# Attention and expert layer on one core: one clearing copy moved from ScalarE to VectorE, and the first 290 items in another order

## Chip, core and metric

The kernel runs on 1 core of one Trainium2 chip. The metric is device time in microseconds (us), the median of several runs, lower is better. Before the change it is 228.75 us (3 runs, 228.53 to 230.53). The engines are named as in the profile: PE (TensorE, matmuls; PEld its weight loads), DVE (VectorE), ACT (ScalarE), POOL (GpSimd) and SP, which only issues DMA transfers.

## What is computed

Causal attention over 4 batches and 8 heads (768 positions, head size 64). Three of the heads ("retrieval": 0, 2, 6) see all earlier positions, the other five only the first 4 positions and a window of 64. The result, 3072 tokens of 512, goes through a layer with a leaky rectifier with one slope per hidden column.

```python
scores = scale * np.matmul(q, k.transpose(0, 1, 3, 2))
...
scores = np.where(mask[None, :, :, :], scores, -1000000000.0)
scores = scores - np.max(scores, axis=-1, keepdims=True)
a = np.exp(scores)
a = a / (np.sum(a, axis=-1, keepdims=True) + 1e-09)
return np.matmul(a, v).astype(np.float32)
...
h = x @ w_in
g = np.maximum(h, 0.0) + alpha * np.minimum(h, 0.0)
return (g @ w_out).astype(np.float32)
```

## The kernel before

The work is cut into 16 attention segments (4 batches by 4 pairs of heads; segment n is pair n % 4 of batch n / 4) and 8 blocks of tokens for the expert layer (two per batch, 512 and 256 tokens). Each piece of work is an *item*: a name in a table with a function. One list, ORDER (line 14), names all 1076 items in the order in which they are emitted; nothing reorders them later. Each engine does its own instructions in that order and waits for the semaphores of what it reads; a bank of PSUM is taken and given back in that order as well. So a name's place in ORDER decides what stands ahead of it on its engine.

What the names mean (n a segment, t a block, i a number):

- `Lq`, `Lk`, `Lv` load q, k, v of a segment on SP's queue (functions load_q, load_k, load_rows, lines 203 to 250; the very first k load and the slopes' load `La` go on ScalarE's queue).
- `Cq`, `Ck`, `Cv` cast what was loaded to bf16. The letters in CQ, CK, CV (line 298) choose the engine: for segments 0 to 3 mostly P (GpSimd), later V (VectorE). `Cv` also copies the first four rows of a segment's values (`sinks`, line 306).
- `Tq`, `Tk` are transposes on TensorE (to_array, lines 354 to 363), `tq`, `tk` copy them out of PSUM into qT and kT (put_q, line 368; put_k, lines 386 to 394): with n of 1 to 3, `tq` on ScalarE and `tk` on VectorE; from 4, both on ScalarE; `tq0.0` on ScalarE, `tq0.1` on VectorE.
- `S` are score matmuls (lines 413 to 501), `s` their exponentials on ScalarE, `m` masks multiplied in on VectorE (from segment 4), `A` the matmuls with the values (line 552), `a` the division on VectorE (lines 562 and 563), `X`, `x` the transposition of the result into xT.
- `P` are the expert layer's first matmuls (line 597; a block's first units are cut in parts, as P0.1.0), `p` the relu on ScalarE (line 602), `g` the product with the slope on VectorE (line 609), `O`, `o` the second matmuls (line 617) and the output.
- `wi0` to `wi7` load w_in on GpSimd's queue (load_w_in, line 692; wi0 and wi1 hold the columns of units 0 to 3, wi6 and wi7 those of units 12 to 15), `wo0` to `wo3` load w_out (line 696).
- Clearing and constants: `zero`, `one`, `busy` and the fills `vz` (a column of values), `kz` (the transposed keys of segment slot i), `qz`, `sz`, `so`, `ro`, `vo`, `nz`, `kfz`, all memsets through line 288; `id` the identity; `idf` its copy in float32 (VectorE), read by `Al` (the transposition of the slopes on TensorE, line 651), whose result `al` turns into factors (line 655); `nms`, `nmr` the masks of segments 0 to 3 and `nr`, `ns` those of later ones (mr_near and ms_near, lines 659 to 677), all on GpSimd; `near0` to `near2` clear parts of the exponentials' buffers.
- `warm0` to `warm8` are matmuls of `busy` with itself whose result nobody reads (32, 3, 14 and six times 4 of them).

The keys' buffer kT_all is cleared by four items, because the streams' layout leaves gaps that the scores read: `kz0` and `kz1` by VectorE, `kz3` by GpSimd, and `kz2`, the slot of the third pair, by a copy on ScalarE from a broadcast zero.

Of the kernel before, what the change touches and what calls it, by code (L numbers as in the profile page):

```python
# [14 lines left out]
busy zero La id warm0 kz3 Lq0.0 sz1 vz2 nms nmr so1 vz0 Lq0.1 Lk1 warm8 warm5 warm3 kz1 qz0 one Lq1 Lk0 Ck0.0 kz2  # L15
Cq0.0 Tq0.0 tq0.0 Tk0.0 qz warm2 Lk2 kz0 tk0.0 Ck1.0 Ck1.1 Cq0.1 Tk1 S0.0.1 s0.0.1 Tq0.1 S0.0.0 Cq1 warm7 Lv0 tk1.0
sz2 vz1 vz3 Tq1 Lq2 Ck0.1 S0.0.2 s0.0.0 tk1.1 Tk0.1 Ck2.1 tq1 S1.1.0 s0.0.2 Ck2.0 warm4 tq0.1 nz0 s1.1.0 Cq2 tk0.1 Cv0
Lk3 S0.1.0 kfz0 Lv1 vo ro0 Ck3.1 s0.1.0 Lq3 Ck3.0 wi1 wi0 Cq3 sz0 idf S1.0.0 so2 Al s1.0.0 so0 al S0.1.1 s0.1.1 Lv2
Tq2 Tk2 tk2.1 tk2.0 S0.1.2 S1.0.1 A0.0 s0.1.2 a0.0 Cv1 A0.1 a0.1 Cv2 s1.0.1 tq2 S1.1.1 nz1 Tk3 S2.0.1 tk3.0 s1.1.1
S2.0.2 X0 s2.0.1 x0 wi6 s2.0.2 wi7 Lv3 Lq5 Tq3 tk3.1 S2.0.0 wi5 m4.0.2 warm6 S2.1.0 A1.0 a1.0 Lk4 s2.0.0 A2.0 S2.1.1  # L20
A1.1 a2.0 tq3 s2.1.0 a1.1 S3.0.0 s2.1.1 s3.0.0 A2.1 a2.1 S3.1.1 X1 S3.0.1 s3.0.1 Lk5 wi4 kfz2 Cv3.0 Cq5 Lk7 wi2 X2
Ck4.0 s3.1.1 S3.1.0 x1 P0.0.0 x2 P0.0.1 A3.0 P0.1.0 P0.1.1 Lk6 Lq4 Lq6 Ck4.1 kfz3 nr Cv3.1 s3.1.0 A3.1 Lv7 Lv5 Lq7
Ck5.0 wi3 a3.0 P0.2.0 Tq5 tq5 P0.3.0 P0.3.1 a3.1 X3 x3 ns kfz1 P0.2.1 Tk4 near2 P1.2 P0.1.2 P0.2.2 P0.0.2 p1.2 p0.1
g0.1 Ck5.1 P1.0 P0.3.2 g1.2 P0.15 tk4.0 p0.2 g0.2 p0.15 wo0 p1.0 Lk8 near0 g0.15 g1.0 ro1 P1.12 P1.14 m12.1.2 p0.0
g0.0 wo1 tk4.1 p1.12 P0.14 g1.12 p0.14 g0.14 P0.13 p0.13 g0.13 P0.11 p1.14 Tk5 Ck7.1 g1.14 P1.10 tk5.0 p0.11 p1.10
Ck6.0 Ck7.0 g0.11 m8.0.2 tk5.1 wo2 Lv6 Lv4 P0.10 P0.8 p0.8 Tk7 g1.10 wo3 Cq4 Lk9 P0.12 P1.8 p0.10 g0.8 p0.12 g0.10 Tq4
P0.6 P0.9 p0.3 Ck6.1 g0.3 tq4 P0.4.0 P0.5.0 Tk6 P0.4.1 p1.8 g1.8 tk7.0 p0.9 g0.9 Cq6 P0.5.1 P0.5.2 p0.5 g0.12 p0.6
tk6.1 P0.4.2 g0.6 g0.5 tk6.0 S4.0.5 P0.7 p0.7 P1.6 g0.7 P1.4 s4.0.5 p0.4 Tq6 m4.1.2 tk7.1 g0.4 Cv5 p1.6 g1.6 O0.1.0
tq6 S4.0.3 O0.2.0 O0.2.1 S5.1.1 S5.0.0 S4.0.1 S6.1.0 m14.0.2 p1.4 g1.4 s5.0.0 O0.1.1 s4.0.3 s4.0.1 O0.2.2 S5.0.2
S5.1.0 S4.0.2 S5.1.2 s6.1.0 m4.0.1 Cv7 O0.3.0 s5.0.2 s5.1.2 s5.1.1 s4.0.2 O0.1.2 s5.1.0 O0.1.3 o0.1 Cq7 Cv4 O0.3.1  # L30
m5.1.0 m8.1.2 m5.0.2 m4.0.3 m5.1.2 S4.0.0 S4.1.4 S5.0.1 S4.0.4 S4.1.0 s4.0.4 s5.0.1 Lk10 m5.0.1 O0.2.3 O0.3.2 Tq7
m5.0.0 o0.2 s4.1.0 m4.0.4 m5.1.1 A5.1 s4.0.0 m4.0.0 a5.1 O0.3.3 tq7 S7.0.0 S7.0.1 S4.1.3 S7.1.1 S6.0.5 S4.1.1 m4.0.5
s4.1.4 o0.3 Lq9 s4.1.3 Ck8 m4.1.3 A5.0 a5.0 X5 s4.1.1 A4.0 s7.0.0 s7.1.1 Lk11 Lq8 s7.0.1 a4.0 s6.0.5 near1 m7.0.0
m7.1.1 m4.1.0 O1.1.0 S7.1.0 S6.0.4 S7.0.2 S4.1.5 S6.0.1 S7.1.2 S6.1.1 O1.1.1 Cv6 s7.1.0 O1.0.0 s4.1.5 m7.0.1 s6.1.1
m4.1.5 m6.1.1 s7.1.2 m6.1.0 s7.0.2 m7.0.2 S6.0.2 S4.1.2 S6.1.2 S6.0.0 s6.0.4 s4.1.2 s6.0.1 s6.1.2 O1.0.1 m6.0.5 m7.1.0
m4.1.1 m4.1.4 m7.1.2 m6.1.2 S6.0.3 A4.1 s6.0.0 m6.0.0 m6.0.1 A7.1 O1.1.2 A6.1 s6.0.3 m6.0.4 m6.0.3 s6.0.2 a4.1 a6.1
A6.0 A7.0 a6.0 O1.1.3 O0.0.0 O0.0.1 O0.0.2 O1.0.2 m10.0.2 O1.0.3 O0.0.3 o0.0 X4 X6 a7.1 a7.0 X7 P2.9 P2.3 p2.9 P3.4
Ck9 Cq9 g2.9 P2.14 p2.14 g2.14 Cq8 p3.4 Lq10 Lq11 Dk8.0 P2.10 p2.10 Dk9.1 o1.0 p2.3 g2.3 g3.4 Dk8.1 P3.2 P3.14 P3.12
# [36 lines left out]
def kernel(  # L75
# [211 lines left out]
    def item(name, fn, *args):  # L287
        I[name] = lambda: fn(*args)  # L288
# [420 lines left out]
    for i in (0, 1):  # L709
        fill(f"kz{i}", kT_all[:, i].bitcast(fp32), 0.0)  # L710
# [137 lines left out]
```

## Time and profile before

| what | value |
| --- | --- |
| median of 3 runs | 228.75 us (228.53 to 230.53) |
| span of the profiled execution, first to last instruction | 227.4 us |
| granted TensorE clock | 1.000 |
| bytes moved by DMA | 37.39 MB |

The profile comes from one execution. Its span is 227.4 us; the time of a run has the launch around it as well, and no own time of the profiled execution is given. Busy time by engine in stretches of 10 us (length, PE, PEld, DVE, ACT, POOL with the number of instructions, clock, DMA share, GB/s):

```profile
0.00:10.00 10.00, 8.30 (x103) 7.54 (x104) 6.58 (x21) 5.34 (x6) 6.62 (x19) 1.00 0.86 243
10.00:20.00 10.00, 9.34 (x151) 8.13 (x149) 8.01 (x25) 8.97 (x13) 8.25 (x15) 1.00 1.11 247
20.00:30.00 10.00, 9.81 (x173) 8.50 (x172) 8.43 (x20) 5.99 (x10) 9.55 (x18) 1.00 1.18 245
30.00:40.00 10.00, 10.00 (x81) 6.92 (x79) 7.12 (x18) 7.88 (x14) 6.96 (x19) 1.00 1.18 248
40.00:50.00 10.00, 10.00 (x73) 6.01 (x72) 8.46 (x19) 9.54 (x23) 0.83 (x1) 1.00 1.21 203
50.00:60.00 10.00, 9.69 (x67) 4.75 (x65) 5.31 (x11) 9.01 (x24) 0.94 (x1) 1.00 1.11 219
```

A row says how much of a stretch each engine worked. Up to some 26 us the four segments of the first batch are loaded, cast, transposed and scored; from 26.8 on the expert layer's matmuls of the first blocks run beside the preparation of segments 4 to 7; the first scores of segment 4 come near 48 us. A line of the timelines gives start, busy time, engine, line, operation, output and input, and in brackets the idle time of the engine ahead of it and what ended it. A line of waits gives who waited for whom, with sum, number and longest.

### The profile page before, as it was taken

The page shows a single profiled execution, that of the slowest core. Times are in us where ns is not written, and L with a number is a line of the kernel's source. Part 1 is how long each engine was busy: PE and PEld are TensorE (multiplying, and loading weights), DVE is VectorE, ACT ScalarE, POOL GpSimd, SP SyncE. Part 2 cuts the span into 40 slices and gives each one's busy share as a digit, 9 for nine tenths or more (in the row PEclk, how much of TensorE's full clock was granted, in tenths as well). Part 3 has the DMA queues.
Part 4 walks back from the last instruction along what each step waited for, and adds up shares of the span by engine and source line. Part 5 has one row for each costly group of instructions (what it writes and reads, how often), then busy time and mean ns, then how long its engine had stood idle before and what let it go on. Part 6 is the DMA issues. An engine that isn't in the chain of part 4 may idle for free.

```text
span 227.4 us, 5240 instructions
## 1 busy us (share of the span) xinstructions
PE 221.6 (97%) x2005; PEld 135.3 (60%) x2005; DVE 150.0 (66%) x394; ACT 140.8 (62%) x285; POOL 46.0 (20%) x91
## 2 busy tenths in 40 slices
PE   8899999999999999999999999999999999999994
PEld 7789876664465657555556455556556555664454
DVE  5779849966379817899799119987586535866000
ACT  3889549999799028477994137787594236563311
POOL 6779995101130001000400001000110110000000
DMA  6999999999999598999969899995821420000213
GB/s 191 314 247 202 281 221 263 210 197 222 216 276 208 94 232 212 164 189 179 255 166 179 209 261 144 211 168 113 127 94 38 116 95 0 0 4 0 89 67 122
DMA packets 95417, 37.39 MB, mean 164 GB/s; under 512 B 82440, under 2 KB 93600, under 8 KB 95392
## 3 DMA queue, kind: packets, MB, share of 16 engines
q1 hardware_dynamic: 89136, 27.73, 61.8%
q0 software_dynamic: 5792, 8.93, 17.7%
q10 hardware_dynamic: 464, 0.40, 0.5%
q8 instruction: 15, 0.25, 0.4%
q14 instruction: 10, 0.08, 0.1%
HBM read 27.71 MB, written 6.29 MB: 150 GB/s over the span
## 4 chain that ended last, share of the span: by engine, by line
PE 90%; ACT 4%; DMA 2%; DVE 2%; issue 1%; ACTq 0%; DVEq 0%
PE P L597 35%; PE P L617 34%; PE P L552 7%; PE P L430 4%; PE P L413 2%; PE P L363 2%; DMA kf<-in_k_dram 2%; PE P L636 2%; ACT neg L602 1%; PE P L501 1%; ACT kT L288 1%; PE P L423 1%; PE P L577 1%; ACT kT L392 1%; DVE qT L368 0%
## 5 line engine op out<-in xcount | busy, mean ns | idle before, releaser
L609 DVE SCALAR_TENSOR_TENSOR g<-neg,oma,P 128x256 bf16<-128x256 f32 (+1 forms) x128 | 71.1, 608 | 36.0 <-ACT neg L602 35.5
L597 PE MATMUL P<-xT,w_in_b 128*128 128x512 bf16 (+1 forms) x512 | 86.5, 326 | 0.0
L617 PE MATMUL P<-w_out_b,g 128*128 128x512 bf16 x368 | 85.4, 379 | 0.0
L602 ACT ACTIVATE neg<-P 128x512 f32<-128x512 f32 x96 | 54.1, 600 | 27.1 <-PE P L597 22.6
L597 PEld LDWEIGHTS <-w_in_b 128*128 128x128 bf16 x512 | 49.5, 98 | 31.7 <-DVE g L609 0.2
L617 PEld LDWEIGHTS <-g 128*128 128x128 bf16 x368 | 33.7, 98 | 37.3 <-issue 1.2
L469 ACT ACTIVATE eR<-P 128x448 bf16<-128x448 f32 (+4 forms) x63 | 37.1, 636 | 5.3 <-PE P L430 2.5
L623 ACT COPY ot<-P 128x512 f32<-128x512 f32 x23 | 13.9, 603 | 37.3 <-PE P L617 32.4
L627 POOL DMA_DIRECT2D out_dram<-ot x18 | 10.3, 573 | 112.5 <-ACT ot L623 112.3
L517 ACT ACTIVATE eS<-P 128x352 bf16<-128x352 f32 x45 | 20.9, 494 | 3.7 <-PE P L430 3.7
L563 DVE TENSOR_TENSOR xn<-P,rcp 128x448 bf16<-128x448 f32 (+1 forms) x32 | 19.4, 608 | 1.1
L528 DVE TENSOR_TENSOR eS<-eS,ms_near 128x352 bf16<-128x352 bf16 x45 | 14.3, 335 | 4.6 <-ACT eS L517 4.5
L479 DVE TENSOR_TENSOR eR<-eR,mr_near 128x128 bf16<-128x128 bf16 (+5 forms) x54 | 11.2, 235 | 4.4 <-ACT eR L469 4.3
L413 PE MATMUL P<-qT,kT 128*128 128x192 bf16 (+14 forms) x68 | 11.3, 250 | 1.2 <-ACT qT L368 0.8
L430 PE MATMUL P<-qT,kT 64*128 64x176 bf16 (+13 forms) x181 | 11.8, 251 | 0.3 <-DVE g L609 0.3
L430 PEld LDWEIGHTS <-kT 64*128 64x128 bf16 x181 | 7.2, 94 | 7.6 <-issue 6.4
L552 PEld LDWEIGHTS <-eS 128*128 128x128 bf16 x260 | 9.6, 97 | 2.3 <-issue 0.6
L552 PE MATMUL P<-vb,eS 128*128 128x65 bf16 x260 | 10.8, 193 | 0.0
L562 DVE RECIPROCAL rcp<-P 128x7 f32<-128x7 f32 (+1 forms) x32 | 6.3, 198 | 6.8 <-PE P L552 6.6
L552 PE MATMUL P<-vb,eR 128*128 128x65 bf16 x276 | 10.1, 192 | 0.0
L552 PEld LDWEIGHTS <-eR 128*128 128x128 bf16 x276 | 9.4, 97 | 1.2
L645 DVE COPY ot<-P 128x128 f32<-128x128 f32 x1 | 0.3, 291 | 14.3 <-PE P L636 14.3
(96 smaller groups left out, 175.2 us busy)
## 6 DMA issues: line engine op xcount, KB each, us to landing
out_dram<-ot POOLq DMA_DIRECT2D x18, 256.0 KB, 3.5
kf<-in_k_dram SPq DMA_DIRECT2D x21, 192.0 KB
qf<-in_q_dram SPq DMA_DIRECT2D x18, 192.0 KB
vf<-in_v_dram SPq DMA_DIRECT2D x14, 196.0 KB
qf<-in_q_dram SPq DMA_DIRECT2D x7, 384.0 KB
vf<-in_v_dram SPq DMA_DIRECT2D x12, 192.0 KB
w_in_b<-in_moe_w_in_dram POOLq DMA_DIRECT2D x8, 256.0 KB, 9.7
w_out_b<-in_moe_w_out_dram POOLq DMA_DIRECT2D x4, 512.0 KB, 14.1
```

Source lines behind the costliest of these rows:

```text
L413: nc.tensor.matmul(to, keys, queries, start=True, stop=stop)
L430: nc.tensor.matmul(to, keys[own], queries[own], start=True, stop=True)
L469: nc.scalar.activation(ebuf[n, hh][:, lo:hi].rearrange("p (x c) -> p x c", x=len(parts)), P[:, got[0]:got[0] + len(parts), 0:(hi - lo) // ...
L517: nc.scalar.activation(slots, sc[:, 0:352].rearrange("p (s c) -> p s c", c=176), AF.Exp, scale=scale)
L528: nc.vector.tensor_tensor(slots, slots, ms_near[:, 0:2, :] if m == 0 else ms_near[:, 1:3, :], op=ALU.mult)
L552: nc.tensor.matmul(pav[:, i, :], e[:, o:o + 128], vv[:, j, hh, 0:D + 1], start=(m == 0), stop=(m == len(terms) - 1))
L563: nc.vector.tensor_tensor(xn[n][:, 0:nt, D * hh:D * hh + D], pav[:, :, 0:D], rcp.to_broadcast([128, nt, D]), op=ALU.mult)
L597: nc.tensor.matmul(psg[:, w * i:w * (i + 1)], w_in_b[:, c, 128 * fb:128 * (fb + 1)], xT[:, c, o:o + w], start=(x == 0), stop=(x == 3))
L602: nc.scalar.activation(neg[t, f], bank(held["P", t, f][0]), AF.Relu, scale=-1.0)
L609: nc.vector.scalar_tensor_tensor(g_buf[t % 2][:, fb, 0:w], neg[t, f][:, c], oma[:, fb:fb + 1], bank(got[0])[:, c], op0=ALU.mult, op1=ALU.add)
L617: nc.tensor.matmul(bank(held["O", t, s][0]), g_buf[t % 2][:, f, 128 * s:128 * (s + 1)], w_out_b[:, f, :], start=(f == 0), stop=(f == 15))
L623: nc.scalar.copy(ot, bank(got[0]))
```

## The change

`kz2` becomes a memset on VectorE like `kz0` and `kz1`. The part of ORDER ahead of `S4.0.5` (the first scores of segment 4), 290 items, is in another order; from `S4.0.5` on the order is the same. The same items are named. The loads on SP's queue keep their order among themselves, and so do the loads on GpSimd's queue. Places that differ, among others: `id` is behind `nz0`; `Cv1` is ahead of `wi1` and `wi0`, and `Cq3` between these; `vz1` is behind `tq0.1` on VectorE and `vz2` behind `al`; `idf` has `vo` ahead of it and no `so`; `Tk2` is ahead of `Al`; the first expert units are P0.1 and P0.3 instead of P0.0; `one`, `nr` and `ns` are last of the 290.

```diff
 ORDER = """
-busy zero La id warm0 kz3 Lq0.0 sz1 vz2 nms nmr so1 vz0 Lq0.1 Lk1 warm8 warm5 warm3 kz1 qz0 one Lq1 Lk0 Ck0.0 kz2
-Cq0.0 Tq0.0 tq0.0 Tk0.0 qz warm2 Lk2 kz0 tk0.0 Ck1.0 Ck1.1 Cq0.1 Tk1 S0.0.1 s0.0.1 Tq0.1 S0.0.0 Cq1 warm7 Lv0 tk1.0
-sz2 vz1 vz3 Tq1 Lq2 Ck0.1 S0.0.2 s0.0.0 tk1.1 Tk0.1 Ck2.1 tq1 S1.1.0 s0.0.2 Ck2.0 warm4 tq0.1 nz0 s1.1.0 Cq2 tk0.1 Cv0
-Lk3 S0.1.0 kfz0 Lv1 vo ro0 Ck3.1 s0.1.0 Lq3 Ck3.0 wi1 wi0 Cq3 sz0 idf S1.0.0 so2 Al s1.0.0 so0 al S0.1.1 s0.1.1 Lv2
-Tq2 Tk2 tk2.1 tk2.0 S0.1.2 S1.0.1 A0.0 s0.1.2 a0.0 Cv1 A0.1 a0.1 Cv2 s1.0.1 tq2 S1.1.1 nz1 Tk3 S2.0.1 tk3.0 s1.1.1
-S2.0.2 X0 s2.0.1 x0 wi6 s2.0.2 wi7 Lv3 Lq5 Tq3 tk3.1 S2.0.0 wi5 m4.0.2 warm6 S2.1.0 A1.0 a1.0 Lk4 s2.0.0 A2.0 S2.1.1
-A1.1 a2.0 tq3 s2.1.0 a1.1 S3.0.0 s2.1.1 s3.0.0 A2.1 a2.1 S3.1.1 X1 S3.0.1 s3.0.1 Lk5 wi4 kfz2 Cv3.0 Cq5 Lk7 wi2 X2
-Ck4.0 s3.1.1 S3.1.0 x1 P0.0.0 x2 P0.0.1 A3.0 P0.1.0 P0.1.1 Lk6 Lq4 Lq6 Ck4.1 kfz3 nr Cv3.1 s3.1.0 A3.1 Lv7 Lv5 Lq7
-Ck5.0 wi3 a3.0 P0.2.0 Tq5 tq5 P0.3.0 P0.3.1 a3.1 X3 x3 ns kfz1 P0.2.1 Tk4 near2 P1.2 P0.1.2 P0.2.2 P0.0.2 p1.2 p0.1
-g0.1 Ck5.1 P1.0 P0.3.2 g1.2 P0.15 tk4.0 p0.2 g0.2 p0.15 wo0 p1.0 Lk8 near0 g0.15 g1.0 ro1 P1.12 P1.14 m12.1.2 p0.0
-g0.0 wo1 tk4.1 p1.12 P0.14 g1.12 p0.14 g0.14 P0.13 p0.13 g0.13 P0.11 p1.14 Tk5 Ck7.1 g1.14 P1.10 tk5.0 p0.11 p1.10
-Ck6.0 Ck7.0 g0.11 m8.0.2 tk5.1 wo2 Lv6 Lv4 P0.10 P0.8 p0.8 Tk7 g1.10 wo3 Cq4 Lk9 P0.12 P1.8 p0.10 g0.8 p0.12 g0.10 Tq4
-P0.6 P0.9 p0.3 Ck6.1 g0.3 tq4 P0.4.0 P0.5.0 Tk6 P0.4.1 p1.8 g1.8 tk7.0 p0.9 g0.9 Cq6 P0.5.1 P0.5.2 p0.5 g0.12 p0.6
-tk6.1 P0.4.2 g0.6 g0.5 tk6.0 S4.0.5 P0.7 p0.7 P1.6 g0.7 P1.4 s4.0.5 p0.4 Tq6 m4.1.2 tk7.1 g0.4 Cv5 p1.6 g1.6 O0.1.0
...
+zero vz3 busy warm5 warm0 nz0 warm8 qz0 nms id qz vz0 sz1 so1 Lq0.0 Lq0.1 nmr Cq0.1 kz1 Lk1 Cq0.0 Tq0.0 Ck1.0 Lq1 La
+Lk0 ro0 Ck0.0 Tk0.0 warm2 Ck1.1 Cq1 kz0 tq0.0 kz2 Lk2 Ck2.0 Tk1 Ck0.1 Ck2.1 tk0.0 S0.0.1 m4.0.2 Lv0 s0.0.1 Tq0.1 Lq2
+S0.0.0 Tq1 tk1.1 kz3 S0.0.2 tk1.0 s0.0.0 sz0 Cv0 ro1 Cq2 kfz0 Lk3 Ck3.1 tq1 warm3 Ck3.0 tq0.1 Tk0.1 s0.0.2 vz1 Lv1 Cv1
+Lq3 S1.1.0 tk0.1 wi1 sz2 warm7 s1.1.0 vo S0.1.0 S1.0.0 Cq3 s0.1.0 Tk2 wi0 warm4 idf Al s1.0.0 tk2.0 S0.1.1 s0.1.1
+S0.1.2 s0.1.2 al A0.0 Tq2 tq2 S1.0.1 vz2 Lv2 s1.0.1 Cv2 A0.1 S1.1.1 a0.0 wi6 Tk3 s1.1.1 wi7 S2.0.1 S2.0.2 tk2.1 s2.0.1
+s2.0.2 a0.1 X0 so0 A1.0 S2.0.0 Tq3 Lv3 tk3.1 Cv3.0 x0 a1.0 so2 S2.1.0 Lq5 tk3.0 wi5 Lk4 warm6 s2.0.0 A2.0 s2.1.0
+S2.1.1 Cq5 A1.1 a2.0 tq3 s2.1.1 S3.0.0 A2.1 s3.0.0 S3.1.1 a1.1 Lk5 X1 s3.1.1 wi4 a2.1 S3.0.1 Lk7 x1 wi2 X2 S3.1.0
+near2 Lk6 x2 Cv3.1 P0.1.0 P0.1.1 Lq4 s3.0.1 A3.0 kfz2 Lq6 Lv7 s3.1.0 P0.3.0 Ck4.1 A3.1 Ck4.0 Lv5 P0.0.0 Lq7 P0.2.0
+P0.2.1 Tq5 a3.0 wi3 a3.1 X3 kfz3 Tk4 P0.3.1 x3 P1.0 P0.0.1 Ck5.1 P0.0.2 tq5 P0.2.2 p0.2 g0.2 P0.1.2 P1.2 p1.0 P0.15
+g1.0 tk4.0 p0.1 g0.1 P0.14 p1.2 wo0 g1.2 Lk8 wo1 P1.14 P0.3.2 p0.15 p0.0 P1.12 g0.15 p1.14 g1.14 g0.0 Ck5.0 p1.12 Tk5
+p0.14 Ck6.0 g0.14 Ck7.1 P0.13 m8.0.2 g1.12 tk4.1 tk5.0 p0.13 g0.13 wo2 P1.10 kfz1 p1.10 P0.10 Ck6.1 Lv6 P0.11 p0.10
+g0.10 Ck7.0 g1.10 tk5.1 p0.11 nz1 P1.8 P0.12 P0.8 p0.3 g0.11 Lv4 P0.6 p0.12 p0.6 wo3 Lk9 g0.3 g0.12 p1.8 g1.8 p0.8 Tk7
+Tk6 Cq4 Tq4 tq4 P0.9 P0.5.0 tk6.1 m12.1.2 g0.6 P0.4.0 P0.4.1 P0.5.1 P0.5.2 p0.9 g0.9 p0.5 tk6.0 Cq6 g0.5 g0.8 tk7.0
+near0 P0.4.2 one nr ns S4.0.5 P0.7 p0.7 P1.6 g0.7 P1.4 s4.0.5 p0.4 Tq6 m4.1.2 tk7.1 g0.4 Cv5 p1.6 g1.6 O0.1.0 tq6
...
-    for i in (0, 1):
+    for i in (0, 1, 2):
         fill(f"kz{i}", kT_all[:, i].bitcast(fp32), 0.0)
-    item("kz2", nc.scalar.copy, kT_all[:, 2].rearrange("p h c -> p (h c)"), zero.to_broadcast([128, 2 * 7 * 128]))
     fill("kz3", kT_all[:, 3].bitcast(fp32), 0.0, nc.gpsimd)
```

## Prediction

> **What bounds the kernel now.** I read the page first, then TensorE's waits in the first 60 us, the chain of waits over the start, the timelines of VectorE, GpSimd and ScalarE up to 60 us, and busy time by stretches. Two lines of the page, busy time and the chain that ended last:
>
> ```profile
> PE 221.6 (97%) x2005; PEld 135.3 (60%) x2005; DVE 150.0 (66%) x394; ACT 140.8 (62%) x285; POOL 46.0 (20%) x91
> PE 90%; ACT 4%; DMA 2%; DVE 2%; issue 1%; ACTq 0%; DVEq 0%
> ```
>
> TensorE sets the time. A reordering that gives it the same 2005 matmuls can win only what TensorE waits. Its waits in the first 60 us, with sum, number and longest:
>
> ```profile
> PE P L687 <- DVE zero L288: 1.1, 1, 1.1
> PE P L413 <- ACT qT L368: 0.8, 2, 0.5
> PE P L413 <- ACT eS L523: 0.4, 2, 0.2
> PE P L430 <- DVE g L609: 0.3, 1, 0.3
> PE P L651 <- DVE eS L288: 0.2, 1, 0.2
> ```
>
> Beside the start itself that is 1.7 us, all there is to win. What sets the first 0.5 us wait is in the chain of waits (start, length, what):
>
> ```profile
> 5.25 0.51 ACT g L328
> 5.77 1.58 ACT kT L288
> 7.35 0.70 ACT qT L368
> 8.05 0.04 issue
> 8.10 0.54 PE P L413 x3
> ```
>
> `kT L288` on ACT is `kz2`: the first scores (8.10) wait for `tq0.0`, which stands behind it. What would be next is in VectorE's timeline (start, busy, instruction, idle before), and ScalarE's load in the middle is in the stretches (PE, PEld, DVE, ACT, POOL):
>
> ```profile
> 6.38 1.01 DVE L386 COPY kT<-P 64x258 bf16<-64x258 bf16 x2 [1.71 <-PE P L361]
> 35.00:55.00 20.00, 19.69 (x142) 11.89 (x141) 16.45 (x34) 19.37 (x42) 3.18 (x5) 1.00 1.16 216
> ```
>
> From 35 to 55 us ScalarE works 19.37 of 20 us: there TensorE's lead is worth only what ScalarE can follow. GpSimd's rows around the first weight loads:
>
> ```profile
> 14.87 0.96 POOL L328 CAST g<-kf 128x384 bf16<-128x384 f32 x2
> 15.77 1.42 POOL L692 DMA_DIRECT2D w_in_b<-in_moe_w_in_dram  x2
> 17.17 0.85 POOL L315 CAST g<-qf 128x768 bf16<-128x768 f32 x1
> 17.94 0.95 POOL L348 CAST vb<-vf 128x896 bf16<-128x896 f32 x1
> 18.96 0.63 POOL L306 COPY vb<-vb 4x192 f32<-4x192 f32 x2
> ```
>
> **The change, part by part.** *kz2 to VectorE.* ScalarE loses a 1.68 us copy; VectorE gains a memset that its twin `kz1` does in 0.81. With the copy gone `tq0.0` can start at 5.77 and end by 6.5; next late is `tk0.0` on VectorE, 6.38 to 7.39, held by the key transposes and not by VectorE, which stood idle 1.71 us before it. The first scores then start at 7.39 plus the 0.05 from 8.05 to 8.10, that is 7.44 instead of 8.10: **-0.66**. Cover: before `tk0.0` VectorE now has `zero`, `vz3`, `busy`, `qz0`, `qz`, `vz0`, `sz1`, `so1`, `kz1` (0.06+0.17+0.11+0.38+0.11+0.17+0.22+0.14+0.81 = 2.2 from 0.90), the query cast (3.30 to 3.66, when its load lands), then `ro0` and two memsets (0.20+1.62): done near 5.5, 0.9 before 6.38. Without cover it would cost up to 0.81.
>
> *idf.* Before, `vo`, `ro0`, `sz2`, `idf` and two `so` stand between the key copies (end 12.53) and the slope transpose (13.99): 1.46 us with 0.30 of issue. After, `sz2`, `vo` and `idf` are left (0.22+0.12+0.71), and TensorE has six transposes and four warm-up matmuls to do ahead of it (chain: 0.34 and 0.22). I take the wait of 0.2 as gone: **-0.2** (bounds 0 and -0.2).
>
> *The scores of segments 0 to 3.* The other 0.25 of qT and the 0.4 of eS depend on which item follows which; new orders make new waits. Bounds 0 and -0.65; I take **-0.2**, nearer to nothing, since ScalarE has the same exponentials to do. So TensorE comes to the first expert matmul, 26.8 before, about 1.1 earlier, at 25.7.
>
> *The stretch bound by ScalarE.* Before, ScalarE's items up to the relu at 50.96 (the one behind the first scores of segment 4) come as relus in runs of one to four with q/k copies between; after, seven relus and later six stand in a row, and five copy groups (`tq4`, `tk6.1`, `tk6.0`, the cast `Cq4`, `tk7.0`) stand behind the six with two relus between. Before, the 16th relu ends at 44.61 and the marked one starts 6.35 later. After, behind the 18th relu stand 0.70 (44.58 to 45.28), 0.80 (45.77 to 46.57), two relus 1.0, 0.70 (50.26 to 50.96), 0.83 and 0.80: 4.85; and the 18th ends at least two units of expert matmuls later than the 16th, each four matmuls of 0.216 (chain: 12 in 2.59), 1.7 in all, and up to one set of transposes, 0.34. 4.85 + 1.7 to 2.1 is 6.6 to 6.9, against 6.35: +0.2 to +0.55. The run of seven can idle more: 7 times (0.86 - 0.55) is 2.2 if nothing is queued ahead. Bounds 0 and +2.2; I take **+0.6**, by the two rows that I could add up.
>
> *Masks late.* `one`, `nr` and `ns` move from near 28 us to just before the scores of segment 4. GpSimd does them in 1.25 (28.06) and 3.47 (30.33 to 33.80); behind `one`, near 51.5 by the row of the product that follows it, they end near 52.8 and 56.3. The first readers are at 56.49 (mr_near) and 59.8 (ms_near). Behind them on GpSimd waits `Cv5`, which starts at 56.11 on a load: nothing, up to 4.7 if the cover failed.
>
> *vz1 and vz2 late.* The value load of segment 1, issued at 9.68, waits for `vz1`, now behind `tq0.1` on VectorE: 10.61 - 0.66 + 0.96 + 0.17 = 11.1, so this load and every load behind it on SP's queue goes out 1.4 later. What hides it is the backlog: a query load issued at 6.26 was cast as it landed, at 13.08, 6.8 us, where the first took 2.5 (0.82 to 3.30): 4.3 queued ahead. Nothing; 1.4 without it.
>
> *GpSimd's queue.* `ident` is made behind `nz0` and `nms`, near 4.0, before its first use at 5.2. The w_out loads go out a few us earlier or as before: nothing, either way. `kz3`, `kfz1`, `nz1` and the warm-up groups only trade places beside other work: nothing. `wi1` and `wi0` are behind `Cv1` now: nothing in my sum, and the first rival.
>
> Sum: -0.66 - 0.2 - 0.2 + 0.6 = -0.46. The span of 227.4 becomes 226.9; the median of 228.75 has 1.35 around that span, so **228.3**. Of the shown runs (228.53, 228.75, 230.53) two lie within 0.2 of each other and one 1.8 above.
>
> **Rivals.** *First expert weights late (slower).* `wi1` and `wi0` were issued at 15.77 and 16.55 and landed 5.8 and 7.3 later. Now `Cv1` with its two small copies (0.95+0.63) stands ahead, and the query cast (0.85) between them. `Cv1` can't start before its load lands, between 13.1 (the query load ahead of it) and 17.2 (the one behind it was cast then), nor before GpSimd is free, 15.8. So `wi0` goes out at 15.8+0.95+0.63+0.65+0.85 = 18.9, or 1.2 later; with 7.3 it lands at 26.2 to 27.4, with the 8.7 of the quickest later one at 27.6 to 28.8. TensorE needs it at 25.7. The price is 0.5 to 3.1, total 228.8 to 231.4, in the middle 230.2. Against: with 5.8 it lands at 24.7 and costs nothing, and the transfers run in a saturated queue (DMA share over 1 from 5 us on), where what starts later needs not end as much later. It decides from a landing at 25.7 on.
>
> *ScalarE follows.* If the run of relus finds its banks full, nothing of the 1.06 is given back: 227.7. For: VectorE, which frees the banks, works only 16.45 of the 20 us. Against: ScalarE's 19.37 of 20.
>
> *The clock rises one period later.* The first 44 warm-up matmuls took 4.20 us, the next 14 took 0.96: TensorE starts at half rate and, from 4.4, 3.3 us after its first matmul, runs at full rate. The first matmul now waits for `busy` as the third memset, 0.2 later, and 40 instead of 44 come before the first transposes. If full rate came only at 7.7, up to half of 3.3 less the 0.26 idle is lost at the first scores, 1.4: 229.7. For it speaks only that the start moves; that the rate rose 3.3 us after the start speaks against. The Trainium skill ("TensorE: Matmul & The Clock Gate", Part 1: The HAM clock gate) says that the window which releases the clock runs freely, about 3.4 us long, so that a later start can miss one; the 3.3 us here agree with its length, and one profile can't show its phase.
>
> *The edit is not what it says:* both programs hold the same items and the same loads, so only the order and one engine differ; no chance.
>
> **Chances.** Forecast 0.50 (its own range 227.6 to 229.2); weights late 0.27; ScalarE follows 0.12; clock 0.06; a wait that I don't see 0.05. 227.2 to 231.2 leaves out a tail of `ScalarE follows` and the upper end of the late weights and the unseen. 1% is 2.3 us, about what a measurement of this kernel can tell from no change. Faster by that needs more than all of TensorE's 1.7 us: 0.06. Slower by it needs the upper third of the late weights, 0.12, or an unseen wait or two together: 0.22. Within: 0.72.
>
> **What would show it.** After: no ScalarE `kT` row at 5.77, the first scores near 7.45, no wait at L651, the first expert matmul near 25.7 with no wait for `w_in_b` (otherwise the first rival), the relu ahead of segment 4's first exponential at 50.4 to 50.6, no VectorE wait on `mr_near` or `ms_near`, first full-rate matmuls near 4.5. A landing of `wi0` after 26, a VectorE stall on a key cast, or a mask that is read late would make the forecast wrong.

## The result, and the profile after

The changed kernel takes 231.45 us (median of 12 runs, 231.09 to 232.94), the kernel before on the same chip 229.72 us (12 runs, 228.53 to 230.64). The ratio is 1.0078, with a 95% interval of 1.0053 to 1.0103: slower by 0.8%, where 228.3 us and no measurable change were forecast. The profiled run took 231.09 us with a span of 229.2 us, against 227.4 before; the granted clock is 1.00 in both. Some single runs of the versions below had a granted clock of 0.991 to 0.993 and took longer, among them three of the splice with the changed start and two with the early masks; by the means without them these two ratios would be near 1.005 and 1.006, not 1.0067 and 1.0073.

Two lines of the page of the changed kernel, busy time and the chain that ended last:

```profile
PE 222.1 (97%) x2005; PEld 134.9 (59%) x2005; DVE 151.6 (66%) x395; ACT 139.3 (61%) x284; POOL 46.4 (20%) x91
...
PE 80%; DMA 8%; ACT 4%; DVE 3%; POOL 2%; issue 1%; ACTq 0%; SPq 0%; POOLq 0%; DVEq 0%
```

TensorE's share of the chain fell from 90 to 80%, and transfers went from 2 to 8%: the way to the end now runs through loads. TensorE's waits in the first 60 us (sum, number, longest):

```profile
PE P L687 <- DVE busy L288: 1.2, 1, 1.2
PE P L597 <- DMA w_in_b<-in_moe_w_in_dram: 0.9, 1, 0.9
PE P L413 <- DVE kT L386: 0.4, 1, 0.4
PE P L430 <- DVE g L609: 0.3, 1, 0.3
PE P L363 <- POOL natm L328: 0.3, 1, 0.3
```

The first expert matmul in TensorE's timelines, before and then after (start, busy, instruction, and in brackets the idle time ahead of it):

```profile
26.80 0.81 PE L597 MATMUL P<-xT,w_in_b 128*128 128x512 bf16 x3
27.02 0.81 PE L597 MATMUL P<-xT,w_in_b 128*128 128x512 bf16 x3 [0.93 <-DMA w_in_b<-in_moe_w_in_dram]
```

The waits on `qT` and on the slopes (L651) are gone, as forecast. New are the first expert matmul's wait for its weights (0.9) and a transposition's for a key cast (0.3). The chain of waits of the same kernel shows where they come from (start, length, what):

```profile
10.02 0.96 DVE qT L368
10.98 0.07 issue
11.05 0.18 DVE vf L288
11.23 0.02 issue
11.24 0.37 SPq L246
11.61 0.04 issue
11.66 4.43 DMA vf<-in_v_dram
16.09 0.03 POOLq L348
16.12 0.08 issue
16.20 0.95 POOL vb L348
17.14 0.05 issue
17.20 0.63 POOL vb L306 x2
17.83 0.73 POOL w_in_b L692
18.56 0.83 POOL g L315
19.39 0.57 POOL w_in_b L692
...
20.65 9.41 DMA kf<-in_k_dram
30.07 0.05 issue
30.12 0.97 POOL natm L328 x2
```

`tq0.1`, then `vz1`, then the value load of segment 1 on SP's queue, its cast `Cv1`, and behind that `wi1`, `Cq3` and `wi0`. `wi0` is issued at 19.32 instead of 16.55 and lands at 26.88 instead of 23.81 (both landings from the transfers' semaphores in the trace). TensorE had finished the scores ahead of the expert matmuls at 26.1.

ScalarE's load in the stretch from 35 to 55 us is still near full, 18.84 of 20 us (length, PE, PEld, DVE, ACT, POOL with instructions, clock, DMA share, GB/s):

```profile
35.00:55.00 20.00, 19.79 (x140) 11.97 (x139) 16.46 (x34) 18.84 (x42) 8.64 (x17) 1.00 1.19 221
```

One more loss was not foreseen. It is in VectorE's timelines, before and then after (start, busy, instruction):

```profile
62.85 0.59 DVE L528 TENSOR_TENSOR eS<-eS,ms_near 128x352 bf16<-128x352 bf16 x2 [1.81 <-ACT eS L517]
64.03 1.36 DVE L528 TENSOR_TENSOR eS<-eS,ms_near 128x352 bf16<-128x352 bf16 x2 [1.75 <-ACT eS L517]
```

Beside the second row, in GpSimd's timeline of the changed kernel:

```profile
64.00 0.94 POOL L348 CAST vb<-vf 128x896 bf16<-128x896 f32 x1 [0.95 <-DMA vf<-in_v_dram]
```

The pair of mask products takes 1.36 us, where before it took 0.59. `Cv4` on GpSimd had started 0.03 earlier. The same steps in both profiles give the account (us from the start of the span):

| step | before | after | difference |
| --- | --- | --- | --- |
| first exponential (L469) | 8.73 | 7.80 | -0.93 |
| last retrieval exponential of segments 0 to 3 | 20.51 | 19.86 | -0.65 |
| first expert matmul (L597) | 26.80 | 27.02 | +0.22 |
| first retrieval exponential of segment 4 | 51.45 | 52.61 | +1.16 |
| a later retrieval exponential, behind these mask products | 65.82 | 67.65 | +1.83 |
| end of the span | 227.4 | 229.2 | +1.8 |

The lead at the start is there. Of it 0.3 is lost by 20 us; 0.9 is lost from there to the first expert matmul, 0.9 up to segment 4 and 0.7 at 64 us; from then on the two profiles run in parallel.

### The profile page after: what moved, and what is told of

Read it like the earlier page. It is cut to its first block, busy times and chain, and to the rows that moved or that the text cites. A ratio compares the mean times of both kernels' runs of the same rounds, so it can differ in the third digit from the quotient of the medians.

```text
span 229.2 us, 5247 instructions
## 1 busy us (share of the span) xinstructions
PE 222.1 (97%) x2005; PEld 134.9 (59%) x2005; DVE 151.6 (66%) x395; ACT 139.3 (61%) x284; POOL 46.4 (20%) x91
## 4 chain that ended last, share of the span: by engine, by line
PE 80%; DMA 8%; ACT 4%; DVE 3%; POOL 2%; issue 1%; ACTq 0%; SPq 0%; POOLq 0%; DVEq 0%
PE P L617 33%; PE P L597 33%; DMA kf<-in_k_dram 6%; PE P L552 6%; PE P L430 4%; DMA vf<-in_v_dram 2%; ACT neg L602 2%; PE P L636 2%; DVE kT L392 1%; DVE eS L528 1%; PE P L423 1%; POOL vb L348 1%; ACT kT L392 1%; POOL w_in_b L692 1%; PE P L363 1%
## 5 line engine op out<-in xcount | busy, mean ns | idle before, releaser
L597 PE MATMUL P<-xT,w_in_b 128*128 128x512 bf16 (+1 forms) x512 | 86.1, 326 | 1.0 <-DMA w_in_b<-in_moe_w_in_dram 0.9
L597 PEld LDWEIGHTS <-w_in_b 128*128 128x128 bf16 x512 | 49.4, 98 | 34.2 <-issue 1.5
L469 ACT ACTIVATE eR<-P 128x448 bf16<-128x448 f32 (+4 forms) x63 | 37.0, 634 | 6.5 <-PE P L462 2.7
L528 DVE TENSOR_TENSOR eS<-eS,ms_near 128x352 bf16<-128x352 bf16 x45 | 15.0, 350 | 4.7 <-ACT eS L517 2.3
```

Source lines behind the costliest of these rows:

```text
L469: nc.scalar.activation(ebuf[n, hh][:, lo:hi].rearrange("p (x c) -> p x c", x=len(parts)), P[:, got[0]:got[0] + len(parts), 0:(hi - lo) // ...
L528: nc.vector.tensor_tensor(slots, slots, ms_near[:, 0:2, :] if m == 0 else ms_near[:, 1:3, :], op=ALU.mult)
L597: nc.tensor.matmul(psg[:, w * i:w * (i + 1)], w_in_b[:, c, 128 * fb:128 * (fb + 1)], xT[:, c, o:o + w], start=(x == 0), stop=(x == 3))
```

## The experiments

Theory: `vz1` behind `tq0.1` and `Cv1` ahead of `wi1`, `wi0` make the first weights late. Rivals: the later order (ScalarE's stretch, the masks), the clock, and a start whose lead is worth nothing. Ratios are to the kernel before on the same chip, with 95% intervals.

**The memset alone.**

```diff
-    for i in (0, 1):
+    for i in (0, 1, 2):
         fill(f"kz{i}", kT_all[:, i].bitcast(fp32), 0.0)
-    item("kz2", nc.scalar.copy, kT_all[:, 2].rearrange("p h c -> p (h c)"), zero.to_broadcast([128, 2 * 7 * 128]))
```

> The kernel before with one edit: kz2 is a memset on VectorE instead of a copy on ScalarE; no item changes its place. Theory (the clearing copy did hold the first scores, and the loss of the changed kernel is all in the other order): the first scores start near 7.45 us instead of 8.10, as they do in the changed kernel (7.37 for the second key copy there against 7.60), and TensorE keeps most of the 0.66, so the span is 226.8 to 227.1 and the ratio to the kernel before 0.997 to 0.9985. Rival (a lead at the start is worth nothing, because loads and the first expert weights set when TensorE goes on): 227.4, ratio 1.000, with the 0.66 back as new waits before 27 us. Second rival (VectorE needs the time and the memset delays the key copies): ratio above 1.001.

Ratio 1.0003 (0.9973 to 1.0033). First scores at 7.61, but then this wait of TensorE:

```profile
PE P L363 <- DVE kT L394: 0.5, 1, 0.5
```

A transposition waits for VectorE's key copies. Of 0.49 at the first exponential 0.15 is left from 16 us on, and that is kept to 66 us. The time shows no gain, which neither excludes nor shows 0.15.

**Which half.** A splice: the first 161 items in the changed order and the rest of the items ahead of `S4.0.5` (they are 291, not 290) as before. And the opposite one.

> A splice: the first 161 items, up to the first expert matmul, in the changed order, and the other items up to the first scores of segment 4 in the order before. kz2 is the memset. It asks in which half the loss lies. Theory (both halves lose: late weights and keys by the first, ScalarE's order by the second): the wait for w_in_b of 0.9 stays, the stretch from 44 to 56 us gives its 0.4 to 0.6 back, and the collision of 0.8 us at 64 us may come or go with the phase: span 227.9 to 228.8, ratio 1.002 to 1.006. If the first half were all of it: 229.2, ratio 1.007 to 1.008. If the second half were all of it: below 227.4, ratio under 1.000.

> The opposite splice: the first 161 items in the order before, with kz2 as a memset on VectorE, then the other items up to the first scores of segment 4 in the changed order. Theory (both halves lose): no wait for w_in_b, the first expert matmul near 26.1 to 26.5 us; the stretch from 44 to 56 us costs 0.4 to 0.6, the masks made late cost nothing by themselves; span 227.0 to 228.0, ratio 0.999 to 1.003. If the second half held all of the loss: 229 or more, ratio above 1.006. If the first half held it all: that of the kernel before with the memset alone, below 227.1, ratio under 0.999.

Changed start: 1.0067 (1.0037 to 1.0096), with a wait of 1.1 for `w_in_b`. Start before: 1.0013 (0.9983 to 1.0042), no such wait. So most of the loss lies in the first half. The second half costs something in the profiles as well. From the first expert matmul to segment 4's first exponential, four profiles with the changed order there and no wait for a load on the way take 24.87 to 24.88 us, and four with the order before take 24.43 or 24.44 (all eight lack the record of that first matmul, so each is 0.2 longer in truth). A lead from the start is not kept by either order: the splice with the start before has 0.91 at the last exponential of segments 0 to 3 (19.60) and 0.13 at segment 4's first (51.32), and a version below with the order before loses 0.78 on the same way.

**Cv1 behind the weights.**

```diff
-vz1 Lv1 Cv1
+vz1 Lv1
...
-Tk2 wi0 warm4
+Tk2 wi0 Cv1 warm4
```

> The changed kernel with one item moved: Cv1, the cast of segment 1's values on GpSimd, stands behind wi0 and no longer ahead of wi1 and wi0. Theory (the first weights are late because their issue waits for this cast, as the chain of waits has it): wi1 goes out near 15.6 us instead of 17.79 and wi0 before 17.5 instead of 19.32, the wait of 0.9 us of the first expert matmul for w_in_b is gone, and about 0.5 to 0.9 us of span with it (228.3 to 228.7, ratio to the kernel before near 1.005). Rival (the key cast natm, which follows a load that landed at 30.07, is late in any case and takes back what is won): no wait for w_in_b, but the wait for natm grows from 0.3 to about 1.2 and the span stays within 0.2 of 229.2, ratio 1.007 to 1.008. Second rival (the transfers are saturated, and weights that start earlier land as late): the wait for w_in_b stays above 0.6.

1.0090 (1.0055 to 1.0125), a miss. The wait for `w_in_b` is gone, but the values' matmuls now wait for this cast:

```profile
PE P L552 <- POOL vb L348: 0.7, 1, 0.7
...
PE P L552 <- POOL vb L306: 0.2, 1, 0.2
```

GpSimd is not short of time there; its queue is held. `Cq3` still stands between `wi1` and `wi0`, and its load comes late, as GpSimd's timeline shows:

```profile
17.80 0.83 POOL L315 CAST g<-qf 128x768 bf16<-128x768 f32 x1 [1.49 <-DMA qf<-in_q_dram]
```

GpSimd stands idle for 1.49 us, `wi0` goes out at 18.57 (the forecast was before 17.5), and `Cv1` starts at 19.20, though its values landed at 16.16.

**vz1 early, and Cq3 behind wi0 as well** (the last pair of lines in the second kernel alone).

```diff
-m4.0.2 Lv0
+m4.0.2 vz1 Lv0
...
-s0.0.2 vz1 Lv1 Cv1
+s0.0.2 Lv1 Cv1
...
-S1.0.0 Cq3 s0.1.0 Tk2 wi0 warm4
+S1.0.0 s0.1.0 Tk2 wi0 Cq3 warm4
```

> The changed kernel with one item moved: vz1, the memset of segment 1's value buffer, stands ahead of Lv0 on VectorE (behind tk0.0) and no longer behind tq0.1. Theory (the 1.4 us for which SP's queue stands still pass through the value load, the cast Cv1 and the weight loads behind it to the first expert matmul): the value load of segment 1 goes out near 9.2 to 9.8 us instead of 11.24 and lands near 15.0; Cv1 starts when GpSimd is free, 15.6, instead of 16.20; wi0 goes out near 18.7 instead of 19.32 and lands near 26.2; the key load behind goes out 1 to 3 us earlier and natm is not waited for. The wait for w_in_b falls from 0.9 to 0.2 to 0.5 and the first relu from 33.41 to 32.6 to 33.0; span 228.2 to 228.9, ratio to the kernel before 1.003 to 1.006. Rival (the backlog of the queue hides the late issue, as the prediction had it): the loads land as in the changed kernel, within 0.3 us, and the span stays at 229.0 to 229.4, ratio 1.007 to 1.008.

> The changed kernel with vz1 ahead of Lv0 and also Cq3, the query cast between the two weight loads on GpSimd, behind wi0. Cv1 stays ahead of wi1. Theory (both the stalled queue and the work between the weight loads make wi0 late): wi1 goes out near 17.2, wi0 near 17.9, landing near 25; no wait for w_in_b at all, no wait for vb, and the first expert matmul starts at 25.3 to 26.2 by the phase of the clock; first relu 32.3 to 32.6; the rest of the way costs what it costs in the changed kernel: span 227.6 to 228.4, ratio 1.000 to 1.004. Rival (weights wait for the transfer queue and not for their issue): the wait for w_in_b stays above 0.6 and the ratio at 1.006 or more.

1.0056 (1.0030 to 1.0081) and 1.0050 (1.0030 to 1.0070). With `Cq3` behind, `wi0` goes out at 18.50 and lands at 27.05, against a forecast near 25 and no sooner than in the changed kernel. In the first of the two the weights land at 28.25 and TensorE waits longer than in the changed kernel, against the forecast: some of the first loads of that run landed up to 1 us later. Both ratios are lower than the changed kernel's 1.0078, but the intervals overlap, so a gain is likely and not shown.

**Both suspects undone, with the later order of either kernel.**

```diff
-m4.0.2 Lv0
+m4.0.2 vz1 Lv0
...
-s0.0.2 vz1 Lv1 Cv1
+s0.0.2 Lv1 wi1 wi0 Cv1
...
-tk0.1 wi1 sz2
+tk0.1 sz2
...
-Tk2 wi0 warm4
+Tk2 warm4
```

> The changed kernel with its two suspects undone: vz1 ahead of Lv0, and wi1, wi0 ahead of Cv1, with Cq3 behind all three on GpSimd. Theory (the start loses by late weight issues and a stalled load queue): wi1 goes out near 15.6, wi0 near 16.3, landing 23.5 to 25; Cv1 runs near 17 and ends in time for the values' matmuls; no wait for w_in_b and none for vb; the first expert matmul starts when TensorE gets there (25.3 to 27 us by the phase at which the clock rises). Mean span of the runs 228.1 to 228.6, against 228.8 with vz1 and Cq3 alone, 229.6 of the changed kernel and 227.9 of the kernel before: ratio 1.001 to 1.003. What is left would be the later order. Rival (what is left lies in the later order alone, the weights are done with at 17.9): 228.8, ratio 1.004 to 1.005.

> The same start with both suspects undone (the first 161 items), and then the order before up to the first scores of segment 4. Theory (start and later order are all that differs, and the memset of kz2 is worth 0 to 0.3): mean span 227.5 to 228.1, ratio 0.998 to 1.001, the first exponential of the late segments 24.4 to 24.7 us after the first expert matmul, as in the kernel before. Rival (the changed start loses by something else as well, such as the order of the scores of segments 0 to 3): 228.4 or more, ratio above 1.002.

1.0024 (0.9996 to 1.0051) and 1.0020 (0.9993 to 1.0046): two thirds of the loss are gone. In the first of the two `wi0` goes out at 15.82 and lands at 24.06, and no expert matmul waits for it. What is left there begins with this wait of TensorE:

```profile
PE P L552 <- POOL vb L348: 0.5, 1, 0.5
```

The cast `Cv2` waits for the values of segment 2, which land at 20.07 (18.99 before), though they were issued at nearly the same time (14.31 and 14.26). The weights went out 0.7 earlier than before; whether they delayed these values is not shown. The wait is 0.9 in the version with the later order before, which missed its forecast of at most 1.001.

**The suspects put into the kernel before.** `vz1` behind `tq0.1`; GpSimd's order `Cv1 wi1 Cq3 wi0`; and both.

```diff
-sz2 vz1 vz3
+sz2 vz3
...
-tq0.1 nz0
+tq0.1 vz1 nz0
...
-Ck3.0 wi1 wi0 Cq3
+Ck3.0 Cv1 wi1 Cq3 wi0
...
-a0.0 Cv1 A0.1
+a0.0 A0.1
```

> The kernel before with vz1 behind tq0.1 on VectorE and nothing else, that is the step of the prediction that was put down at nothing. Theory: SP's queue stands still, the value load goes out near 11.8 instead of 9.68 and all loads behind it land 1 to 2 us later, the key loads of the later segments more; but the weights are ahead of Cv1 here, so wi0 stays near 16.5, and only the key cast natm could be late: mean span 227.9 to 228.3, ratio 1.000 to 1.002. If the late loads alone held the loss: ratio 1.004 or more, with TensorE waiting for natm or vb. If the backlog hides it all: ratio 0.999 to 1.001 and landings within 0.3 of those before.

> The kernel before with GpSimd's order of the changed kernel around the first weights (Cv1, wi1, Cq3, wi0) and nothing else; vz1 stays early. Theory (each suspect costs by itself, the two share one price, the landing of wi0): Cv1 starts when GpSimd is free, near 15.6 to 16, wi0 goes out near 18.5 to 19 instead of 16.55 and lands near 26 to 27.5, against a first expert matmul at 26.8: a wait of 0 to 0.6, mean span 0.2 to 0.8 above that of the kernel before in the same session, ratio 1.001 to 1.0035. Rival (vz1 is all of it): ratio 0.999 to 1.001. If Cv1 held all of it: 1.0045 or more.

> The kernel before with both suspects put in and nothing else: vz1 behind tq0.1 on VectorE, and on GpSimd the order Cv1, wi1, Cq3, wi0 as in the changed kernel. kz2 stays a copy on ScalarE. Theory (these two edits make the first weights late whatever the rest): the value load goes out near 11.8 instead of 9.68, wi0 near 19.5 to 20 instead of 16.55 and lands near 27 to 28; the first expert matmul waits 0.5 to 1.2 for w_in_b; mean span 228.5 to 229.1, ratio 1.003 to 1.006. Rival (in the order before TensorE comes to the experts late enough): no wait for w_in_b above 0.3, ratio 0.999 to 1.002.

`vz1` alone 1.0033 (1.0007 to 1.0059), `Cv1` and `Cq3` alone 1.0073 (1.0053 to 1.0094), both 1.0049 (1.0020 to 1.0078). All cost, and each of the first two more than expected. GpSimd's order by itself costs about as much as the whole change (its medians, 230.70 against 229.28, are 0.6% apart). They do not add up; the intervals overlap. The chain of waits of the kernel before with GpSimd's order alone:

```profile
15.98 0.95 POOL vb L348
16.92 0.05 issue
16.98 0.64 POOL vb L306 x2
17.61 0.73 POOL w_in_b L692
18.34 0.00 issue
18.34 0.65 POOL g L315
18.99 0.12 issue
19.11 8.39 DMA w_in_b<-in_moe_w_in_dram
27.50 0.35 issue
27.85 0.59 PE P L597 x2
```

`wi0` is issued at 19.11 and lands at 27.50, and TensorE, done at 26.6, waits. (Some records of matmuls are missing here, the first of this group among them.) In its profile every later step is 0.83 to 0.84 behind the kernel before, up to the end: 228.3 against 227.4. That run was the quickest of its twelve (229.96), so the profile shows only half of what the ratio has. With `vz1` alone the profile shows no such wait and a span of 227.5; its ratio says that other runs lose more, and where they lose it is not shown.

Over all 19 profiles the cause can be read from two numbers, the landing of `wi0` and the start of the first expert matmul. In the eight in which `Cv1` stands ahead of `wi1` and `wi0`, the matmul starts 0.14 behind the landing, or 0.35 where its first record is missing: the weights release it every time. In the eleven others it starts 0.8 to 3.3 behind, so the weights are there first.

**The masks.** `one`, `nr`, `ns` made early in the changed kernel, and late in the kernel before (there as the last three ahead of `S4.0.5`).

```diff
-X3 kfz3 Tk4 P0.3.1 x3
+X3 kfz3 one nr Tk4 P0.3.1 ns x3
...
-near0 P0.4.2 one nr ns S4.0.5
+near0 P0.4.2 S4.0.5
```

> The changed kernel with one, nr and ns (the masks of the later segments) back near 32 to 38 us, where the kernel before makes them; nothing else is moved. Theory (the late masks cost nothing: their readers start 3 us after they end): first relus as in the changed kernel, the exponential behind the relus of segment 4 near 52.6, span 229.0 to 229.4, ratio 1.007 to 1.008; the key and query casts on GpSimd and the w_out loads come 3 to 5 us later, which may add 0.3. Rival (GpSimd's 3.6 us of mask work between 52 and 56 us slows VectorE or ScalarE there, and so makes the stretch from 44 to 56 us longer): the exponential near 52.0 and the span 228.5 to 228.8, ratio 1.004 to 1.006.

> The kernel before with one, nr and ns as the last items ahead of the first scores of segment 4, as in the changed kernel, and nothing else. Theory (nobody waits for a mask: they end near 52 and 55.5, their first readers start at 56.5 and 59.8): ratio 0.998 to 1.001, and key casts and w_out loads 1 to 4 us earlier on GpSimd. Rival (a mask is read late): VectorE waits on mr_near or ms_near, ratio above 1.002. Second rival (the earlier loads and casts shorten the way to the first exponential of segment 4): ratio under 0.998.

1.0073 (1.0040 to 1.0105): nothing is won by making them early. In the kernel before, making them late gives 1.0028 (1.0000 to 1.0056), above the forecast of at most 1.001. No reader waits for a mask there; TensorE does wait 1.5 at 45 us for a query cast, whose load landed at 44.11 instead of 41.94. The w_out loads went out 1.4 earlier (32.95 against 34.34), since the masks no longer stand ahead of them, but they did not make that load late: it took 16.2 us against 15.9 and had been issued at 27.89 instead of 26.04, before any mask of the kernel before and any w_out load. SP's queue was behind already at 22 us. So the profile shows no cost of the late masks; whether the ratio holds one stays open.

**Cv4 away from the mask products.**

```diff
-o0.1 Cq7 Cv4 O0.3.1
+o0.1 Cq7 O0.3.1
...
-m5.0.0 o0.2 s4.1.0
+m5.0.0 o0.2 Cv4 s4.1.0
```

> The changed kernel with Cv4, the cast of segment 4's values on GpSimd, behind the output o0.2 on GpSimd's queue; nothing else is moved. In the profiles with the changed start this cast starts at 64.00 to 64.53 us, and a mask multiplication of VectorE that starts while it runs takes 1.36, 1.18 or 1.07 us where it takes 0.59 or 0.33 alone (0.59 and 0.33 in the three profiles in which the cast starts after it). Theory (VectorE is held until GpSimd's cast ends, and TensorE waits for the mask): the pair takes 0.59 again, TensorE's wait of 0.5 for eS is gone, and the span is 0.4 to 0.65 shorter than that of the changed kernel: 228.5 to 228.9, ratio 1.0045 to 1.0065. Rival (the multiplication is slow for another reason, for instance what it reads): 1.2 to 1.4 as before, span 229.2, ratio 1.007 to 1.008. A second miss is possible: the cast, now near 65.5, holds the divisions behind it instead, with the same span.

1.0088 (1.0060 to 1.0115), so no gain in time: the second miss that was named. The pair takes 0.59 again, but the cast, now at 65.17, holds the next product instead. VectorE's timeline:

```profile
63.68 0.59 DVE L528 TENSOR_TENSOR eS<-eS,ms_near 128x352 bf16<-128x352 bf16 x2 [1.75 <-ACT eS L517]
...
65.22 0.98 DVE L479 TENSOR_TENSOR eR<-eR,mr_near 128x128 bf16<-128x128 bf16 x1 [0.56 <-ACT eR L469]
```

0.98, where this form takes 0.21 to 0.23 in the other rows, and it ends just behind the cast (65.17 + 0.94). The hold is shown; avoiding it needs another place.

**Keeping the lead.** The kernel before with the memset behind `kz0`, and the small memsets ahead of the first key copy.

```diff
-Ck0.0 kz2 Cq0.0
+Ck0.0 Cq0.0
...
-Lk2 kz0 tk0.0
+Lk2 kz0 kz2 vz1 sz2 vz3 tk0.0
...
-tk1.0 sz2 vz1 vz3 Tq1
+tk1.0 Tq1
```

> The kernel before with kz2 as a memset on VectorE behind kz0, and with vz1, sz2 and vz3 right behind it, ahead of the first key copy instead of between the copies of segments 0 and 1; nothing else. Theory (the copy did hold the first scores, and the lead was eaten at 10 us by a transposition that waits for VectorE's key copies, 0.47 to 0.5 in the two profiles with the memset alone): first scores at 7.0 to 7.7 by the phase of the clock, that wait below 0.15, the first expert matmul 0.5 to 1.0 earlier than in the kernel before at the same phase; mean span 0.3 to 0.8 below that of the kernel before in the same session, ratio 0.9965 to 0.999. Rival (the time is set elsewhere: the weights and loads, or ScalarE from 35 us on, take the lead back): ratio 0.9985 to 1.0015, with new waits between 20 and 55 us. Second rival (VectorE is too full ahead of the first key copy): that copy later than 0.2 behind its transposes, ratio above 1.001.

0.9998 (0.9969 to 1.0027). The wait on the key copies is gone and the lead is 0.78 up to 27 us. Then a query cast is late, in GpSimd's timeline:

```profile
28.31 0.82 POOL L315 CAST natq<-qf 128x768 bf16<-128x768 f32 x1 [3.22 <-DMA qf<-in_q_dram]
```

In the kernel before it starts at 25.54. TensorE waits 0.5 for it, and at segment 4's first exponential the version is 0.18 behind the kernel before. No version tried beats the kernel before.

**The warm-up.** The start before's 44 warm-up matmuls in the kernel with both suspects undone (the edit shown), and the changed 40 in the kernel before (its opposite).

```diff
-zero vz3 busy warm5 warm0 nz0 warm8
+busy zero vz3 warm5 warm0 nz0 warm8 warm3
...
-tq1 warm3 Ck3.0
+tq1 Ck3.0
```

> The changed kernel with both suspects undone (vz1 ahead of Lv0; wi1, wi0 ahead of Cv1 and Cq3) and with the warm-up of the kernel before: busy is the first memset, ahead of zero and vz3, and four of the warm-up matmuls (warm3) stand ahead of the first transposes again, so 44 run from 1.07 us instead of 40 from 1.24. Theory of the clock (the later and shorter warm-up lets the full rate begin later in some runs): full rate 3 to 4.8 us after the first matmul, mean span 0.3 to 0.5 below the 0.67 that the mended kernel lay above the kernel before, ratio 1.000 to 1.0015. Rival (the scatter of the clock is chance): ratio 1.002 to 1.003 as without this edit.

> The kernel before with the warm-up of the changed one and nothing else: zero and vz3 are memset ahead of busy, and four of the warm-up matmuls (warm3) come at 11.9 us, beside those that stand there, instead of ahead of the first transposes. Theory of the clock: first matmul near 1.24, 40 warm-up matmuls, full rate in some runs 5.5 us or more after the first matmul, mean span 0.2 to 0.5 above the kernel before, ratio 1.001 to 1.002. Rival (chance): full rate as before, ratio 0.9995 to 1.0005. The interval of such a run is about 0.003 to each side, so the time alone will hardly decide; the profile adds one phase.

1.0028 (1.0004 to 1.0052), no gain against 1.0024; and 1.0014 (0.9995 to 1.0033). In the first, TensorE waits 1.6 for the values of segment 2. So the warm-up is not shown to hold the remaining quarter of a per cent. It is not excluded either: the intervals reach 0.0024 to 0.0027 to each side, and the second run leaves room for up to 0.3%.

## Why the prediction was wrong, step by step

The span was forecast at 226.9 and is 229.2 in the profile. The 2.3 between them are the wait for the weights (0.9), TensorE's later arrival there (26.1 instead of 25.7), the wait for `natm` (0.3) and the held mask products at 64 us (0.7).

*The failed step: GpSimd's queue ("wi1 and wi0 are behind Cv1 now: nothing in my sum, and the first rival").* The rival came true. It had `wi0` out at 18.9, landing at 26.2 to 28.8, and deciding from 25.7 on; it went out at 19.32, landed at 26.88, and TensorE waited 0.9. In the kernel before, these casts ahead of the weights cost 1.0073 by themselves, so the nothing in the sum was the error. The rival's total (230.2) lay 1.5 above the median that the forecast started from, and the ratio makes it 1.8; that they are so near is in part luck, since the weights cost 0.9 and not its middle of 1.8, and the rest came from losses that stood in no rival (0.28 for `natm`, 0.7 at 64 us). What was wrong is the reason for ranking it second, that in a saturated queue "what starts later needs not end as much later". In the 19 profiles `wi0` lands 7.0 to 9.0 us after its issue, wherever that is. The quickest flight of the profile, 5.8, belonged to `wi1` and was no bound for `wi0`.

*vz1 late ("Nothing; 1.4 without").* Wrong in part. The late issue was right (11.24 against 11.1 forecast), and so was the backlog for the load itself: it lands 0.3 later than before (16.09 against 15.80). The step looked no further than that load. In the changed kernel the key load for segment 4 goes out at 20.65 instead of 19.12 and lands at 30.07 instead of 26.60; with `vz1` alone in the kernel before it goes out at 19.99 and lands at 28.16. So `vz1` can account for part of that lateness; SP's queue also waits 0.7 and 0.4 us there for copies and casts on GpSimd. Alone the edit gave 1.0033.

*kz2 (-0.66).* The mechanism was right (first scores at 7.17 in the profile after, 7.44 forecast) and the size was a single profile's. There the first key cast on ScalarE starts at 5.25; in four other profiles with the copy it starts at 4.59 to 4.87, and the first scores at 7.51 to 8.03. Copy: 7.80 on average of five profiles; memset in nearly the same order: 7.40 of three (7.02 to 7.61). So about 0.4, and in time nothing (1.0003, 0.9998), because the next waits take it back.

*idf (-0.2).* Right: the wait at L651 is gone. *Scores (-0.2).* Not right: TensorE was ready for the experts at 26.1, 0.4 later than forecast, with a new wait of 0.4 for a key copy (L386) on the way.

*ScalarE's stretch (+0.6).* Right in the profile: the 18th relu ends at 47.24 and the marked one starts at 52.12, 4.88 later, where 4.85 was added up. From the first expert matmul to segment 4 the changed kernel loses 0.94, of which 0.28 is the wait for `natm`, so 0.66; the eight profiles above give 0.44. The rival that ScalarE follows, with nothing of the lead given back, did not come. In time the second half is not told apart from nothing (1.0024 with it, 1.0020 without).

*Masks (nothing).* Right for their readers, and no profile shows another cost; the ratio of 1.0028 leaves one open.

*The clock (0.06).* Full rate came at 3.98 in the profile after, earlier than the 4.43 of the kernel before. Other profiles had it as late as 7.2. *The end at 64 us* was in no rival: VectorE's product and GpSimd's cast came together because TensorE's work slipped by 1.2 and the cast's load by 0.4.

Two sums are slightly off. The six terms behind the 18th relu add up to 4.83. And 17.2 lies 1.4 behind 15.8, not 1.2, so the range of the late weights should end 0.2 later. Neither changes the ranking.

## What to carry to other kernels

When a reordering puts anything ahead of a load's issue, follow every later issue on that queue to its reader, and price the landing by the same transfer's own flight; a full queue is no proof that lateness is absorbed. A lead on the bounding engine is worth what the loads behind it allow, so ask for each gained microsecond which transfer is due next. Read a wait at the very start from several profiles, since the first load and the clock move it by more than the edit.

## What the runs showed of the hardware that was not expected

The rise of the clock scatters widely. Warm-up matmuls start 107 ns apart and then 56; the change comes 3.0 to 4.8 us after the first matmul in nine profiles with the warm-up before, and 2.7 to 6.0 in ten with the changed one. Five of these ten lie above 4.8 and none of the nine, which hints at the warm-up as a cause and does not show it. TensorE's timelines of two kernels with the same warm-up; first the changed one (start, busy, instruction):

```profile
1.25 3.68 PE L687 MATMUL P<-busy 128*128 128x128 bf16 x40 [1.25 <-DVE busy L288]
```

The one with `vz1` early and `Cq3` behind:

```profile
1.24 4.45 PE L687 MATMUL P<-busy 128*128 128x128 bf16 x40 [1.24 <-DVE busy L288]
5.62 1.49 PE L361 MATMUL P<-ident,g 128*64 128x128 bf16 x12
```

In the second all 40 run at half rate, and the twelve transpositions take 1.49, where they take 0.86 at full rate (`vz1` alone in the kernel before). The Trainium skill ("TensorE: Matmul & The Clock Gate", Part 1: The HAM clock gate) has a free-running window of 3.4 us and a transition that varies by about half a us either way; that the moment differs from profile to profile agrees, but the scatter here, 2.7 to 6.0, is three times as wide.

A product of VectorE that starts during a cast of GpSimd ends only after the cast: 1.36, 1.18 and 1.03 instead of 0.59, and 0.98 instead of 0.21 to 0.23. The Trainium skill ("SBUF — State Buffer", SBUF: two separate sides) calls this an exclusive lock on a port pair that the two share, held for a whole instruction; these rows agree. The casts take their usual 0.93 to 0.94 us in all four, where a sharing of bandwidth should have made them longer too.

One load can take microseconds longer in another version though it is issued at the same time. The query load whose cast starts as it lands was issued at 17.30 in the kernel before, at 17.66 with the memset alone and at 17.32 in the version that keeps the lead; the cast started at 25.54, 26.13 and 28.31. These are three programs with one profile each, so whether runs of one program differ as much is not shown.
